# A three-stage kernel: chunk 1's router placed behind chunk 2's first product, and the loads around it reordered

## The chip, the cores and the metric

The kernel runs on one core of one Trainium2 chip. The metric is the device time of one execution in microseconds (us). The core has five engines that run side by side and wait for each other by semaphores: TensorE (matmul, "PE" in the rows), VectorE (DVE), ScalarE (ACT), GpSimd (POOL) and SyncE (SP), which here does nothing but issue DMAs. Each engine takes its instructions strictly in order, so an instruction that waits holds up all that stand behind it on its engine.

## The reference, cut to what matters

Three stages follow each other on 2304 tokens of width 512 (4 sequences of 576).

```python
# 1. attention with a window of 128 and a slope per head (8 heads of 64)
scores = q @ k.T / 8 - slope * |i - j|, masked to 0 <= i - j < 128
x = softmax(scores) @ v                      # 2304 x 512
# 2. a dense layer
h = x @ w_in                                 # 512 x 2048
y = (h * clip(h + 3, 0, 6) / 6) @ w_out      # 2048 x 512
# 3. a mixture of 8 experts, one expert per token
logits = normalise(y) @ normalise(expert_emb).T / tau
e = argmax(logits);  gate = softmax(logits)[e]
out[token] = gate * (relu(y @ w1[e]) @ w2[e])
```

Outputs are float32. The dense weights w_in and w_out come as float64, which the kernel turns into float32 itself, from their two words.

## The kernel before

The tokens are cut into nine chunks of 256 (chunk 0 to 8). For each chunk the kernel computes attention in four units (a unit is two heads of one chunk, so chunk c has units 4c to 4c+3), the first dense product in eight blocks (`gemm1`, tiles h_ps), the second product of those blocks (`gemm2`, tiles y_ps), and then the chunk's router (class `Route`). The experts come last, in the second half of the run; the change doesn't touch them.

The 16 blocks of dense weights ("pieces", 1 MB each as stored, tiles wst) are loaded and converted at the start: ScalarE and VectorE make float32 of each (`piece_clamp`, `piece_words`), and split it for later chunks into a rounded part (`piece_high`, ScalarE) and the rest (`piece_low`, VectorE, L355). Chunk 0 is computed with the plain weights (L702, L759), all later chunks as three passes over split operands (L715, L768).

Units 8 and on take their keys, queries and values by small DMAs: `load` issues those of k and q (L557), `load_v` those of v (L577, L579). VectorE turns the keys and the queries (`turn_k`, kT, and `turn_q`, qT), ScalarE scales qT, TensorE makes the scores (L605), VectorE and ScalarE the softmax, TensorE turns the weights (L644), GpSimd masks them (L659), TensorE multiplies by v (acc, L670).

A chunk's router for chunks 0 to 6 doesn't use TensorE for the logits. `rows` copies the two halves of y to ys and stores them, `norms` squares them on ScalarE and takes the root on GpSimd (rn). `spread` loads the normalised embeddings of four experts, repeated over all 128 partitions (en_all, 1 MB, L823), and `dots` runs one VectorE instruction for each expert and half of the tokens (L829, 16 in a chunk). There is one free buffer for en_all, so the second `spread` of a chunk waits for the first eight dots, and the first of the next chunk for the last eight. `choose` then takes the best expert, `ranks` counts tokens per expert on TensorE (two small matmuls into rk, L875 and L876), and `place` scatters the tokens' numbers into slots by two indirect DMAs of GpSimd (L891).

Two things set the order. Up to the end of chunk 1 a planner (`plan`) writes it out by hand: tasks with an engine, a cost, a rank, the tasks they need and the buffers they take; at each time it starts the ready task of the lowest rank, and the program takes that order on PE, ACT, DVE and SP. From then on a table of steps (`at(step, ...)`) gives TensorE's order, and a scheduler places the rest around it. Step 16.97 (`FIRST[0]`) is the first product of chunk 2, and each block takes 1.91 steps. `ends(c)` is the step at which chunk c's router begins; choose stands 10.9 steps behind it, ranks and place 12.28 (`DOTS`). For chunk 1 it returned `begins(1)`, which is 16.97 - 8 x 1.91 = 1.69. Chunk 0's router is in the planner up to its dots; its choose stands at step 16.97 and its ranks at 18.97.

In the planner, the loads of units 8 to 13 are tasks ("qk", n) with all 16 issues of a unit's keys and queries in one, and ("v", n) with its 6 or 8 issues. Those of unit 8 may begin behind the issue of piece 12 or 13, and their ranks (60 to 65) stand among those of the last pieces. `issue spread` for chunk 0 has rank 0.

Of the kernel before, what the change touches and what calls it, by code (L numbers as in the profile page):

```python
# [9 lines left out]
F32 = mybir.dt.float32  # L10
# [6 lines left out]
SP = mybir.EngineType.SP  # L17
# [35 lines left out]
UNIT_8 = (95.0, 150.0, 96.0)  # L53
EMBED = (96.0, 97.0)
SOFT_1, DOTS_0 = 250.0, 2000.0
UNIT_LOADS = ((60.0, 60.1), (61.0, 61.1), (62.0, 62.1), (63.0, 63.1), (64.0, 64.1), (65.0, 65.1))
FIRST = (16.97, 1.91, 3.35)


# [38 lines left out]
def tile_kernel(  # L98
# [13 lines left out]
    nc = tc.nc  # L112
# [27 lines left out]
    raw = right.enter_context(tc.tile_pool(name="raw", bufs=2, side="right"))  # L140
# [34 lines left out]
    for p in range(NP):  # L175
# [369 lines left out]
    class Unit:  # L545
        def __init__(self, n):
            self.c, self.p = divmod(n, NP)
            self.h0 = 2 * self.p
            self.pt, self.pp, self.nm = {}, {}, {}

        def load(self):
            def get(src, g, n, nm):
                t = raw.tile([128, n // 32, 32], F32, tag=nm, name=nm)
                for b, s, o, m in pieces_of(g, n):
                    for h in range(2):
                        for f in range(2):
                            nc.sync.dma_start(  # L557
                                out=t[64 * h + 32 * f:64 * h + 32 * f + 32, o // 32:(o + m) // 32, :],
                                in_=src[b, self.h0 + h, s:s + m, 32 * f:32 * f + 32].rearrange("(t j) i -> j t i", j=32),
                            )  # L560
                return t

            g = self.c * CH
            self.kr = get(k, g - 128, CH + 128, "kr")
            self.qr = get(q, g, CH, "qr")

        def load_v(self):
            self.vr = t = raw.tile([128, 3, 128], F32, tag="vr", bufs=V_BUFS, name="vr")
# [579 lines left out]
    n_early = EARLY_CHUNKS * NP  # L1148
# [7 lines left out]
    def begins(c, i=0):  # L1156
        return FIRST[0] + FIRST[1] * (8 * (c - 2) + i)
# [3 lines left out]
        return GROUPS[0] + GROUPS[1] * n if n < 5 else GROUPS[2] + 2 * FIRST[1] * (n - 5)  # L1161

    def ends(c, i=NF2 - 1):
        return 0.0 if c == 0 else begins(c) if c == 1 else begins(c, i) + FIRST[2]

    for c in range(2, NCH):
        for i in range(NF2):
# [6 lines left out]

    def plan():
        tasks, free = {}, {"bank": 8, "w": 17, "st": 3, "f": 5, "nm": 2, "sm": 2, "rs": 2, "ph0": 2, "ph1": 2, "g": 2,
                           "gl": 2, "u": 1, "raw": 2, "vr": 2, "kT": 1, "qT": 1, "p": 2, "part": 1, "both": 1}

        def task(name, engine, cost, rank, needs=(), takes=(), gives=(), fn=None, args=(), lag=0.12):
            assert name not in tasks, name  # L1180
# [57 lines left out]
        task(("constants",), "SP", 1.6, CONST_RANK[0], [("issue", "st", 8)], ["w"], ["w"], constants)  # L1238
        for n in range(n_early, AHEAD_UNITS):
            u = units[n]  # L1240
            for x, y in enumerate(("qk", "v") if n <= last_unit else ("qk",)):
                load((y, n), (0.6, 0.3)[x], UNIT_LOADS[n - n_early][x], ["raw" if x == 0 else "vr"], (u.load, u.load_v)[x], needs=[("issue", "st", 12 + x)] + ([("issue", y, n - 1)] if n > n_early else []), issues=(16, 6)[x])

        def step(name, engine, cost, rank, needs, takes, gives, fn, *args, lag=0.12):
            task(name, engine, cost, rank, needs, takes, gives, fn, args, lag)
# [4 lines left out]
        for n in range(n_early, last_unit + 2):  # L1250
            u, key = units[n], ("unit", n)
            first = n == n_early
            r = UNIT_8[0] if first else SOFT_1 + n
            step(key + ("kT",), "DVE", 0.5, r, [("qk", n)], ["kT"], [], u.turn_k)
            step(key + ("qT",), "DVE", 0.4, r, [key + ("kT",)], ["qT"], ["raw"], u.turn_q)
            step(key + ("scale",), "ACT", 0.45, r, [key + ("qT",)], [], [], u.scale_q)
            if n > last_unit:
                continue
            r = UNIT_8[2] if first else SOFT_1 - 10
            for h in range(2):  # L1260
                step(key + ("soften", h), "DVE", 0.85, r + 0.1 * h, [key + ("scores",)], ["p", "nm"], ["bank"], u.soften, h)
                step(key + ("expo", h), "ACT", 0.95, r + 0.2 + 0.1 * h, [key + ("soften", h)], [], ["nm"], u.expo, h)
                step(key + ("norm", h), "DVE", 0.75, r - 1, [key + ("expo", h)], ["rs"], ["rs"], u.normalise, h)
                step(key + ("unload", h), "ACT", 0.34, r - 2, [key + ("flip",)], ["ph%d" % h], ["bank"] * h, u.unload_p, h)
                step(key + ("select", h), "POOL", 1.75, r, [key + ("unload", h)], [], [], None)
            if n < last_unit:
                step(key + ("part",), "ACT", 0.36, r - 3, [key + ("values",)], ["part"], ["bank"], u.part)
                step(key + ("both",), "DVE", 0.38, r - 3, [key + ("part",)], ["both"], ["bank", "part"], u.both)
                step(key + ("keep",), "ACT", 0.36, r - 4, [key + ("both",)], [], ["both"], u.keep, lag=0.6)
                step(key + ("kept",), "DVE", 0.38, r - 4, [key + ("keep",)], [], [], None)  # L1270
# [15 lines left out]
        for x in ORDER_1:  # L1286
            before = line[-1:]
            if x == "u":
                i, at_up = at_up, at_up + 1
                name = ("up 1", i)  # L1290
                step(name, "PE", 2.88, 1000, before + [("low", ip["i", i])] + [("unit", kk, "keep") for kk in range(n_early)], ["bank"], [], gemm1, 1, i, lag=0.0)
                r = SOFT_1 - 20 + i
                step(("done 1", i), "X", 0.0, 0, [name], [], [], None, lag=0.2)
                step(("relu 1", i), "ACT", 0.62, r, [("done 1", i)], ["u"], [], relu, 1, i)
                step(("gate 1", i), "DVE", 0.62, r, [("relu 1", i)], [], ["bank"], gate, 1, i)
                step(("gh 1", i), "ACT", 0.56, r, [("gate 1", i)], ["g"], [], split_hi, 1, i)
                step(("gl 1", i), "DVE", 0.64, r, [("gh 1", i)], ["gl"], ["u"], split_lo, 1, i)
            elif x == "d":
                i, at_down = at_down, at_down + 1
                name = ("down 1", i)  # L1300
                step(name, "PE", 2.76, 1000, before + [("low", ip["o", i]), ("gl 1", i)], [] if i else ["bank", "bank"], ["g", "gl"], gemm2, 1, i, lag=0.0)
            else:
                k = int(x)
                n = n_early + k
                name = ("group flips", k)
                needs = before + both_of(("unit", n - 1, "norm")) + ([("en", "scale")] if k == 1 else [])
                step(name, "PE", 0.53 + 0.4 * (k == 1), 1000, needs, ["bank"] * (2 if k == 1 else 1), ["p", "p"] + ["f"] * (k == 1), flips_of, k, lag=0.0)
                step(("unit", n - 1, "flip"), "X", 0.0, 0, [name], [], [], None, lag=0.2)
                if k == 1:
                    step(("en", "keep"), "DVE", 0.17, SOFT_1, [name], [], ["bank"], keep_embed)  # L1310
                needs = [name, ("unit", n, "scale")] + ([("unit", n - 2, "kept")[:2] + ("select", h) for h in range(2)] + [("v", n - 2)] if k > 1 else [])
                name = ("group", k)
                step(name, "PE", 0.8 if k == 1 else 1.47, 1000, needs, ["bank"] * (2 if k == 1 else 4), ["kT", "qT"] + ["ph0", "ph1", "vr"] * (k > 1), group_of, k, lag=0.0)
                step(("unit", n, "scores"), "X", 0.0, 0, [name], [], [], None, lag=0.2)
                if k > 1:
                    step(("unit", n - 2, "values"), "X", 0.0, 0, [name], [], [], None, lag=0.1)
            line.append(name)
# [8 lines left out]
            step(("row store", t), "SP", 0.55, 0.0, [("row", t)], [], [], route_0.store, t)  # L1326
        step(("norms",), "ACT", 1.5, 1900.0, [("row", 1)], ["f"], [], route_0.norms)
        for x in range(2):
            step(("issue spread", x), "SP", 0.55, 0.0, [("en", "store")] + ([("dots", NE // 2 - 1)] if x else []), ["w"], [], route_0.spread, x)
            step(("spread", x), "DMA", 4.8, 0.0, [("issue spread", x)], [], [], None, lag=1.0)  # L1330
        for e in range(NE):
            x, y = divmod(e, NE // 2)
# [338 lines left out]
```

## Time and profile before

| what | value |
|---|---|
| time, median of 3 runs | 801.19 us (801.0 to 805.07) |
| time of the profiled execution | 807.43 us |
| its span, first to last instruction | 805.7 us |
| PE busy | 752.0 us, 93% of the span |
| DVE busy | 525.1 us, 65% |
| ACT busy | 384.1 us, 48% |
| mean granted TensorE clock | 0.976 |

The profile comes from one execution, so what it shows is measured against 807.43 us and not against the median. TensorE is busy almost throughout; the page's 40 slices show it at 7 to 9 tenths in the first fifth, then one slice at 0 and two at 8, and 9 in all but the last of the rest. Read such a profile from TensorE's gaps: a gap on the engine that is busy 93% of the time is time lost, and the view of waits says which gaps are long and what ended them. The timelines of the other engines then show why that came late.

### The profile page before, as it was taken

What the parts mean: (1) busy time and instruction counts of PE and PEld (TensorE: products, weight loads), DVE (VectorE), ACT (ScalarE), POOL (GpSimd) and SP (SyncE); (2) the same over time, 40 slices, a digit from 0 to 9 for tenths busy, and PEclk for the clock granted to TensorE, in tenths of its full rate; (3) what the DMA queues carried; (4) which work ended last, traced back from release to release, by engine and by line L of the source; (5) the groups of instructions that cost most, each with busy time, mean ns of one, the idle gap of its engine ahead of it and who ended that gap; (6) DMA issues with size and microseconds to landing.
All of it is one profiled execution on the core that took longest, in us unless ns stands there. A gap on an engine that the chain in (4) does not pass through costs nothing.

```text
span 805.7 us, 16007 instructions
## 1 busy us (share of the span) xinstructions
PE 752.0 (93%) x5740; PEld 661.9 (82%) x5740; DVE 525.1 (65%) x1528; ACT 384.1 (48%) x896; POOL 191.1 (24%) x349
## 2 busy tenths in 40 slices
PE   7999889908899999999999999999989999999995
PEld 5666568807788888888888888987979999999994
DVE  4999789866347866958777677247727537536621
ACT  6858566423345454454554544326625525535510
POOL 3010022312223224233242332113124132132200
PEclk9999989967999999999999999999999999999998
DMA  9976422262423435244334340029358565455300
GB/s 229 337 272 189 94 51 45 68 173 46 112 35 102 123 69 149 49 110 128 97 86 125 83 136 4 28 31 324 119 159 274 181 216 190 145 201 187 107 26 27
DMA packets 159110, 103.20 MB, mean 128 GB/s; under 512 B 119419, under 2 KB 135931, under 8 KB 157232
## 3 DMA queue, kind: packets, MB, share of 16 engines
q1 hardware_dynamic: 155280, 92.53, 40.2%
q0 software_dynamic: 3744, 9.58, 3.4%
q8 instruction: 47, 0.77, 0.4%
q14 instruction: 39, 0.32, 0.2%
HBM read 87.71 MB, written 14.47 MB: 127 GB/s over the span
## 4 chain that ended last, share of the span: by engine, by line
PE 61%; DMA 15%; issue 11%; DVE 4%; SPq 4%; POOL 3%; ACT 1%; POOLq 0%; DVEq 0%; ACTq 0%
PE h_ps L715 20%; PE y_ps L768 19%; PE ps_u L1038 6%; PE ps_o L1062 4%; DMA out_dram<-ob,ids 3%; DMA kr<-in_k_dram 3%; DMA wst<-in_moe_w_in_dram 3%; PE ps_z L1120 3%; PE acc L670 3%; PE sc_ps L605 2%; DMA ids<-slots 2%; DMA slots<-pays,dest 2%; DMA xg<-ybuf,ids 2%; PE ps_pt L644 1%; SPq L557 1%
## 5 line engine op out<-in xcount | busy, mean ns | idle before, releaser
L715 PEld LDWEIGHTS h_ps<-xs,w_i 128*128 128x128 f32 x1536 | 194.4, 193 | 5.8 <-issue 0.8
L715 PE MATMUL h_ps<-xs,w_i 128*128 128x256 f32 x1536 | 197.2, 285 | 0.0
L768 PE MATMUL y_ps<-w_o,gh 128*128 128x512 f32 x512 | 162.9, 399 | 0.5 <-ACT gh L739 0.5
L659 POOL TENSOR_SCALAR_AFFINE_SELECT ph<-ph 64x128 f32<-64x128 f32 x224 | 90.5, 404 | 194.5 <-ACT ph L651 153.2
L768 PEld LDWEIGHTS y_ps<-w_o,gh 128*128 128x128 f32 x512 | 91.6, 188 | 24.5 <-issue 6.3
L1038 PE MATMUL ps_u<-x,w_e 128*128 128x280 f32 (+5 forms) x768 | 105.4, 294 | 0.0
L162 DVE TENSOR_TENSOR w_e<-st,w_e 128x1024 fp32r<-128x1024 f32 x64 | 76.5, 1217 | 38.4 <-ACT w_e L161 38.4
L1038 PEld LDWEIGHTS ps_u<-x,w_e 128*128 128x128 f32 x768 | 100.5, 189 | 0.2
L768 PE MATMUL y_ps<-w_o,gl 128*128 128x512 f32 x256 | 100.1, 391 | 0.4 <-DVE gl L745 0.4
L829 DVE CUSTOM_DVE_ANT_0 junk<-ys,en_all 128x512 f32<-128x512 f32 x112 | 77.3, 690 | 30.4 <-DMA en_all<-en_rows 18.7
L725 ACT ACTIVATE u<-h_ps,three 128x512 f32<-128x512 f32 x72 | 49.1, 682 | 75.4 <-PE h_ps L715 54.2
L1062 PE MATMUL ps_o<-hs,w_e 128*128 128x280 f32 (+4 forms) x576 | 78.5, 295 | 0.0
L735 DVE SCALAR_TENSOR_TENSOR u<-u,h_ps 128x512 f32<-128x512 f32 x72 | 49.3, 684 | 43.8 <-ACT u L725 42.9
L1062 PEld LDWEIGHTS ps_o<-hs,w_e 128*128 128x128 f32 x576 | 76.6, 188 | 0.0
L161 ACT CAST w_e<-st 128x1024 fp32r<-128x1024 f32 x64 | 65.5, 1048 | 17.1 <-DMA st<-in_moe_w_dram 6.3
L739 ACT CAST gh<-u 128x512 fp32r<-128x512 f32 x64 | 39.7, 620 | 59.4 <-DVE u L735 58.8
L745 DVE TENSOR_TENSOR gl<-u,gh 128x512 fp32r<-128x512 f32 x64 | 45.7, 714 | 27.7 <-ACT gh L739 27.0
L628 ACT ACTIVATE pt<-pt,nm 128x128 f32<-128x128 f32 x112 | 44.1, 395 | 31.4 <-DVE pt L621 31.3
L768 PEld LDWEIGHTS y_ps<-w_o,gl 128*128 128x128 f32 x256 | 48.1, 188 | 11.9 <-DVE gl L745 1.2
L1137 POOL DMA_INDIRECT out_dram<-ob,ids x23 | 30.3, 1315 | 111.8 <-DVE ob L1136 100.3
L1046 ACT ACTIVATE hs<-ps_u 128x280 fp32r<-128x280 f32 (+5 forms) x64 | 25.6, 403 | 45.4 <-PE ps_u L1038 44.8
L891 POOL DMA_INDIRECT slots<-pays,dest x18 | 19.8, 1098 | 95.8 <-DVE u L735 36.4
(185 smaller groups left out, 1007.9 us busy)
## 6 DMA issues: line engine op xcount, KB each, us to landing
st<-in_moe_w_dram SPq DMA_DIRECT2D x32, 512.0 KB
st<-in_moe_w_dram SPq DMA_DIRECT2D x16, 1024.0 KB
en_all<-en_rows SPq DMA_DIRECT2D x14, 1024.0 KB
wst<-in_moe_w_in_dram SPq DMA_DIRECT2D x8, 1024.0 KB
wst<-in_moe_w_out_dram SPq DMA_DIRECT2D x8, 1024.0 KB
ybuf<-ys SPq DMA_DIRECT2D x18, 256.0 KB
out_dram<-empty SPq DMA_DIRECT2D x18, 256.0 KB
kr<-in_k_dram SPq DMA_DIRECT2D x48, 48.0 KB
```

Of the source, the lines that this page charges most:

```text
L161: nc.scalar.copy(hi, src)
L162: eng.tensor_tensor(out=lo, in0=src, in1=words(hi), op=ALU.subtract)
L628: nc.scalar.activation(out=x, in_=x, func=AF.Exp, scale=-1.0, bias=nm[:, j:j + 1], accum_out=sums[h][:, j:j + 1])
L659: nc.gpsimd.affine_select(out=out, in_=x, compare_op=ALU.is_gt if out is prev else ALU.is_ge, fill=0.0, base=0, pattern=[[0, 2], [-1 if ou ...
L715: nc.tensor.matmul(hp[:, f, :], lhsT=w[:, a, kk, f * 128:(f + 1) * 128], rhs=xs[:, b, kk, :], start=(n == 0), stop=(n == 3 * KD - 1),)
L725: nc.scalar.activation(out=u, in_=hp, func=AF.Relu, bias=three, scale=1.0)
L735: V.scalar_tensor_tensor(out=u, in0=u, scalar=6.0, in1=h_t[c, i], op0=ALU.min, op1=ALU.mult)
L745: V.tensor_tensor(out=gl, in0=g, in1=words(gh), op=ALU.subtract)
L768: nc.tensor.matmul(y_t[c][t], lhsT=g[a][:, f, t * 128:(t + 1) * 128], rhs=w[:, b, f, :], start=(i == 0 and f == 0 and n == 0), stop=(i == ...
L829: V.tensor_tensor_reduce(out=self.junk, in0=self.ys[t], in1=self.en[:, e % (NE // 2), :], scale=1.0, scalar=0.0, op0=ALU.mult, op1=ALU.add ...
L1038: nc.tensor.matmul(ps, lhsT=w[:, a, kk, (f % 2) * 128:(f % 2) * 128 + 128], rhs=x[:, b, kk, c0:c1], start=(n == 0), stop=(n == 3 * KD - 1),)
L1062: nc.tensor.matmul(ps, lhsT=ws_t[j, 4 + f // 2][:, a, f % 2, d * 128:(d + 1) * 128], rhs=hs[:, b, f, 0:width(j)], start=(n == 0), stop=(n ...
```

## The change

There are three edits. First, `ends(1)` returns `begins(2)`, 16.97, in the place of `begins(1)`, 1.69: chunk 1's rows, norms, spreads, dots, choose, ranks and place stand 15.28 steps later in the table. Second, `Unit.load` is cut into `load_k` and `load_q`, and the planner has three tasks for each unit (keys, queries, values), with costs of their own and buffers kr and qr counted apart; unit 8's may begin behind the issue of pieces 12 and 13 as before, those of all later units behind piece 15, the last. Third, the spreads of chunk 0 have rank 90 in the place of 0 and also need piece 15 to be issued.

```diff
-UNIT_LOADS = ((60.0, 60.1), (61.0, 61.1), (62.0, 62.1), (63.0, 63.1), (64.0, 64.1), (65.0, 65.1))
+UNIT_LOADS = (80.0, 81.0, 82.0, 83.0, 84.0, 85.0)
...
+        def load_k(self):
+            self.kr = self.get(k, self.c * CH - 128, CH + 128, "kr")
+
+        def load_q(self):
+            self.qr = self.get(q, self.c * CH, CH, "qr")
...
     def ends(c, i=NF2 - 1):
-        return 0.0 if c == 0 else begins(c) if c == 1 else begins(c, i) + FIRST[2]
+        return 0.0 if c == 0 else begins(2) if c == 1 else begins(c, i) + FIRST[2]
...
-            for x, y in enumerate(("qk", "v") if n <= last_unit else ("qk",)):
-                load((y, n), (0.6, 0.3)[x], UNIT_LOADS[n - n_early][x], ["raw" if x == 0 else "vr"], (u.load, u.load_v)[x], needs=[("issue", "st", 12 + x)] + ([("issue", y, n - 1)] if n > n_early else []), issues=(16, 6)[x])
+            for x, y in enumerate(("rk", "rq", "rv") if n <= last_unit else ("rk", "rq")):
+                late = ("issue", "st", 12 + x if n == n_early else 15)
+                load((y, n), (0.43, 0.29, 0.15)[x], UNIT_LOADS[n - n_early] + 0.1 * x, [("kr", "qr", "vr")[x]], (u.load_k, u.load_q, u.load_v)[x], needs=[late] + ([("issue", y, n - 1)] if n > n_early else []), issues=(8, 8, 6)[x])
...
-            step(("issue spread", x), "SP", 0.55, 0.0, [("en", "store")] + ([("dots", NE // 2 - 1)] if x else []), ["w"], [], route_0.spread, x)
+            step(("issue spread", x), "SP", 0.55, 90.0, [("en", "store"), ("issue", "st", 15)] + ([("dots", NE // 2 - 1)] if x else []), ["w"], [], route_0.spread, x)
```

What this moves shows in the order of the instructions. TensorE behind chunk 1's last product (the first two rows are its last matmuls; rk is a router, ps_pt, acc and sc_ps are one group of attention), before:

```order
L768 MATMUL y_ps<-w_o,gh 128x512 x2
L768 MATMUL y_ps<-w_o,gl 128x512
L875 LDWEIGHTS earlier
L875 MATMUL rk<-oh,earlier 128x16
L876 LDWEIGHTS ones
L876 MATMUL rk<-seen,ones 128x16
L715 MATMUL h_ps<-xs,w_i 128x256 x48
...
L644 MATMUL ps_pt<-ident,pt 128x2x64 x4
```

and in the change:

```order
L773 MATMUL y_ps<-w_o,gh 128x512 x2
L773 MATMUL y_ps<-w_o,gl 128x512
L720 MATMUL h_ps<-xs,w_i 128x256 x48
L880 LDWEIGHTS earlier
L880 MATMUL rk<-oh,earlier 128x16
L881 LDWEIGHTS ones
L881 MATMUL rk<-seen,ones 128x16
L649 MATMUL ps_pt<-ident,pt 128x2x64 x4
L675 MATMUL acc<-ph,vr 64x192 x4
L675 MATMUL acc<-ph,vr 64x128 x4
L675 MATMUL acc<-ph,vr 64x64 x4
L610 MATMUL sc_ps<-kT,qT 64x192 x8
```

Before, the first rk is chunk 1's; the second, chunk 0's, follows the 48 matmuls of chunk 2's first two blocks. In the change only one router stands here, chunk 0's, behind the 48 matmuls, and chunk 1's follows some 60 rows later, behind five more blocks of h_ps, five of y_ps and three groups of attention. The sc_ps of this group are unit 14's.

SyncE from the store of the normalised embeddings to the last piece, before:

```order
L285 DMA en_rows<-en 8x512
L823 DMA en_all<-en_rows 128x2048
L315 DMA wst<-in_moe_w_out_dram 128x2x1024
L315 DMA wst<-in_moe_w_in_dram 128x4x512
L315 DMA wst<-in_moe_w_out_dram 128x2x1024
L557 DMA kr<-in_k_dram 32x6x32 x8
...
L315 DMA wst<-in_moe_w_in_dram 128x4x512
...
L315 DMA wst<-in_moe_w_out_dram 128x2x1024
...
L579 DMA vr<-in_v_dram 128x64 x2
L315 DMA wst<-in_moe_w_out_dram 128x2x1024
```

and in the change:

```order
L285 DMA en_rows<-en 8x512
L315 DMA wst<-in_moe_w_out_dram 128x2x1024
L315 DMA wst<-in_moe_w_in_dram 128x4x512
L315 DMA wst<-in_moe_w_out_dram 128x2x1024
L562 DMA kr<-in_k_dram 32x6x32 x8
L315 DMA wst<-in_moe_w_in_dram 128x4x512
...
L315 DMA wst<-in_moe_w_out_dram 128x2x1024
...
L584 DMA vr<-in_v_dram 128x64 x2
L315 DMA wst<-in_moe_w_out_dram 128x2x1024
```

Before, the spread of 1 MB stood ahead of the last six pieces, and unit 8's 16 key and query loads, its eight value loads and all 24 loads of unit 9 ahead of the last of them. In the change the spread stands 13 rows behind the last piece, behind the loads of units 9, 10 and 11, and only unit 8's loads are left ahead of it, cut in three between the last pieces.

VectorE around the gate u of chunk 0's last block and chunk 1's first gl (w_i and w_o are the low parts of split pieces, L333 to L339 the conversion of the last piece), before:

```order
L333 TENSOR_SCALAR w_909<-w_909 128x1024
L589 STREAM_TRANSPOSE qT<-qr 128x256
L335 SCALAR_TENSOR_TENSOR w_909<-wst,w_909 128x1024
L355 TENSOR_TENSOR w_i<-w_364,w_i 128x1024
L339 SCALAR_TENSOR_TENSOR w_909<-wst,w_909 128x1024
L735 SCALAR_TENSOR_TENSOR u<-u,h_ps 128x512
L355 TENSOR_TENSOR w_i<-w_505,w_i 128x1024
L355 TENSOR_TENSOR w_o<-w_724,w_o 128x1024
L735 SCALAR_TENSOR_TENSOR u<-u,h_ps 128x512
L355 TENSOR_TENSOR w_o<-w_550,w_o 128x1024
L745 TENSOR_TENSOR gl<-u,gh 128x512
```

and in the change:

```order
L740 SCALAR_TENSOR_TENSOR u_994<-u_994,h_ps_875 128x512
L355 TENSOR_TENSOR w_i_923<-w32_424,w_i_923 128x1024
L355 TENSOR_TENSOR w_i_1013<-w32_364,w_i_1013 128x1024
L355 TENSOR_TENSOR w_i_1016<-w32_505,w_i_1016 128x1024
L355 TENSOR_TENSOR w_o_1019<-w32_664,w_o_1019 128x1024
L355 TENSOR_TENSOR w_o_1050<-w32_550,w_o_1050 128x1024
L355 TENSOR_TENSOR w_i_1061<-w32_550,w_i_1061 128x1024
L740 SCALAR_TENSOR_TENSOR u_1068<-u_1068,h_ps_1021 128x512
L355 TENSOR_TENSOR w_i_1071<-w32_664,w_i_1071 128x1024
L355 TENSOR_TENSOR w_o_1074<-w32_747,w_o_1074 128x1024
L750 TENSOR_TENSOR gl_1112<-u_1068,gh_1077 128x512
```

Before, the last piece's conversion stood directly ahead of the last gate, five low parts stood somewhere ahead of it and three between it and gl. In the change the conversion is some 20 rows further ahead, three low parts stand ahead of the gate and eight between it and gl.

VectorE ahead of unit 14's queries, in the change (junk is a dot of chunk 1, lg its sum, u and gl are chunk 2's second block, both, xs unit 12's):

```order
L740 SCALAR_TENSOR_TENSOR u<-u,h_ps 128x512
L834 ISA junk,lg<-ys,en_all 128x512
L834 ISA lg 128x1
...
L689 TENSOR_TENSOR both<-acc,part 128x256
L750 TENSOR_TENSOR gl<-u,gh 128x512
L590 STREAM_TRANSPOSE kT<-kr 128x384
L893 CAST dest<-den 128x2
L162 TENSOR_TENSOR xs<-both,xs 128x256
L834 ISA junk,lg<-ys,en_all 128x512
...
L594 STREAM_TRANSPOSE qT<-qr 128x256
```

Four dots of chunk 1 stand ahead of unit 14's keys and four more between its keys and its queries. Before, its keys stood behind eight dots and its queries behind eleven, and TensorE had not begun chunk 2 by then.

## Rows read from the trace of the kernel before

**Rows 1.** windows view: stretch, length, then PE PEld DVE ACT POOL busy, clock, DMA share, GB/s
```profile
103.00:162.00 59.00, 58.54 (x472) 48.05 (x472) 52.35 (x151) 34.05 (x85) 16.90 (x41) 0.95 0.24 56
162.00:215.00 53.00, 26.74 (x215) 23.68 (x216) 29.19 (x123) 13.95 (x41) 10.99 (x32) 0.74 0.41 98
```

**Rows 2.** the waits view, TensorE, first 260 us: total, times, longest
```profile
PE rk L875 <- DVE oh L866: 23.6, 1, 23.6
PE y_ps L759 <- DVE u L735: 4.7, 1, 4.7
PE acc L670 <- POOL ph L659: 3.1, 2, 1.8
```

**Rows 3.** timeline of TensorE, 160 to 216 us: start, us, what, wait before
```profile
161.16 0.39 PE L768 MATMUL y_ps<-w_o,gl 128*128 128x512 f32 x1
...
185.43 8.12 PE L715 MATMUL h_ps<-xs,w_i 128*128 128x256 f32 x48
...
193.46 0.64 PE L644 MATMUL ps_pt<-ident,pt 128*128 128x128 f32 x4
...
195.49 0.73 PE L768 MATMUL y_ps<-w_o,gh 128*128 128x512 f32 x2
...
203.99 3.03 PE L715 MATMUL h_ps<-xs,w_i 128*128 128x256 f32 x24
206.86 0.60 PE L644 MATMUL ps_pt<-ident,pt 128*128 128x128 f32 x4
...
214.22 0.73 PE L768 MATMUL y_ps<-w_o,gh 128*128 128x512 f32 x2
```

**Rows 4.** timeline of VectorE, 160 to 184 us
```profile
160.42 0.42 DVE L684 TENSOR_TENSOR both<-acc,part 128x256 f32<-128x256 f32 x1
...
164.73 0.17 DVE L868 TENSOR_SCALAR rn<-rn 128x2 f32<-128x2 f32 x1 [1.27 <-POOL rn L818]
...
177.82 0.69 DVE L829 CUSTOM_DVE_ANT_0 junk<-ys,en_all 128x512 f32<-128x512 f32 x1 [4.92 <-DMA en_all<-en_rows]
...
178.56 0.69 DVE L829 CUSTOM_DVE_ANT_0 junk<-ys,en_all 128x512 f32<-128x512 f32 x1
```

**Rows 5.** timeline of SyncE's DMA issues, 51 to 173 us
```profile
51.40 0.32 SPq L823 DMA_DIRECT2D en_all<-en_rows  x1
...
53.59 11.11 SPq L557 DMA_DIRECT2D kr<-in_k_dram  x8
...
70.05 0.39 SPq L315 DMA_DIRECT2D wst<-in_moe_w_in_dram  x1
...
76.23 0.38 SPq L315 DMA_DIRECT2D wst<-in_moe_w_out_dram  x1
...
90.79 0.38 SPq L315 DMA_DIRECT2D wst<-in_moe_w_out_dram  x1
...
172.44 0.34 SPq L823 DMA_DIRECT2D en_all<-en_rows  x1
```

**Rows 6.** timeline of TensorE, 90 to 112 us
```profile
90.68 3.60 PE L759 MATMUL y_ps<-w,u 128*128 128x512 f32 x8
...
94.78 3.22 PE L715 MATMUL h_ps<-xs,w_i 128*128 128x256 f32 x24
102.74 6.47 PE L759 MATMUL y_ps<-w,u 128*128 128x512 f32 x8 [4.74 <-DVE u L735]
...
111.92 0.63 PE L768 MATMUL y_ps<-w_o,gh 128*128 128x512 f32 x2
```

**Rows 7.** timeline of VectorE, 97 to 104 us
```profile
97.66 0.69 DVE L333 TENSOR_SCALAR w<-w 128x1024 int32<-128x1024 int32 x1 [4.96 <-ACT w L323]
...
102.00 0.68 DVE L735 SCALAR_TENSOR_TENSOR u<-u,h_ps 128x512 f32<-128x512 f32 x1
102.60 1.22 DVE L355 TENSOR_TENSOR w_i<-w,w_i 128x1024 fp32r<-128x1024 f32 x1
103.73 1.22 DVE L355 TENSOR_TENSOR w_o<-w,w_o 128x1024 fp32r<-128x1024 f32 x1
```

More of the change, by code (lines that the diff above doesn't have):

```diff
@@ L549, in __init__, with get @@
             self.pt, self.pp, self.nm = {}, {}, {}
-        def load(self):
[L552 to L565, printed above, removed]
+        def load_k(self):
+            self.kr = self.get(k, self.c * CH - 128, CH + 128, "kr")
+        def load_q(self):
+            self.qr = self.get(q, self.c * CH, CH, "qr")
+        def get(self, src, g, n, nm):
+            t = raw.tile([128, n // 32, 32], F32, tag=nm, name=nm)
+            for b, s, o, m in pieces_of(g, n):
+                for h in range(2):
+                    for f in range(2):
+                        nc.sync.dma_start(
+                            out=t[64 * h + 32 * f:64 * h + 32 * f + 32, o // 32:(o + m) // 32, :],
+                            in_=src[b, self.h0 + h, s:s + m, 32 * f:32 * f + 32].rearrange("(t j) i -> j t i", j=32),
+                        )
+            return t
+        def load(self):
+            self.load_k()
+            self.load_q()
         def load_v(self):
@@ L1176, in plan @@
         tasks, free = {}, {"bank": 8, "w": 17, "st": 3, "f": 5, "nm": 2, "sm": 2, "rs": 2, "ph0": 2, "ph1": 2, "g": 2,
-                           "gl": 2, "u": 1, "raw": 2, "vr": 2, "kT": 1, "qT": 1, "p": 2, "part": 1, "both": 1}
+                           "gl": 2, "u": 1, "kr": 2, "qr": 2, "vr": 2, "kT": 1, "qT": 1, "p": 2, "part": 1, "both": 1}
         def task(name, engine, cost, rank, needs=(), takes=(), gives=(), fn=None, args=(), lag=0.12):
@@ L1253, in plan @@
             r = UNIT_8[0] if first else SOFT_1 + n
-            step(key + ("kT",), "DVE", 0.5, r, [("qk", n)], ["kT"], [], u.turn_k)
-            step(key + ("qT",), "DVE", 0.4, r, [key + ("kT",)], ["qT"], ["raw"], u.turn_q)
+            step(key + ("kT",), "DVE", 0.5, r, [("rk", n)], ["kT"], ["kr"], u.turn_k)
+            step(key + ("qT",), "DVE", 0.4, r, [key + ("kT",), ("rq", n)], ["qT"], ["qr"], u.turn_q)
             step(key + ("scale",), "ACT", 0.45, r, [key + ("qT",)], [], [], u.scale_q)
@@ L1310, in plan @@
                     step(("en", "keep"), "DVE", 0.17, SOFT_1, [name], [], ["bank"], keep_embed)
-                needs = [name, ("unit", n, "scale")] + ([("unit", n - 2, "kept")[:2] + ("select", h) for h in range(2)] + [("v", n - 2)] if k > 1 else [])
+                needs = [name, ("unit", n, "scale")] + ([("unit", n - 2, "kept")[:2] + ("select", h) for h in range(2)] + [("rv", n - 2)] if k > 1 else [])
                 name = ("group", k)
```

## The prediction

> **What bounds the kernel now.** I read the page first: TensorE is busy 93% of the span, so time is lost where it is not. The windows view then cuts the run into stretches [rows 1]. From 103 to 162 us, chunk 1's products, TensorE is busy 58.54 of 59 us; from 162 to 215, the start of chunk 2, 26.74 of 53, at a granted clock of 0.74. The view of waits names the gaps [rows 2]: 23.6 us for the router's rk, once, 4.7 us for a gate (u) of chunk 0's last block, 3.1 us for masked weights (ph). The reader is to see that three waits hold nearly all that can be won here.
>
> The large one, on the timeline: chunk 1's last product ends at 161.16 + 0.39 = 161.55, and the next 48 matmuls start at 185.43, behind the router [rows 3]. VectorE shows what the router waits for [rows 4, 5]: chunk 0's last dot ends at 160.42; only then can chunk 1's first spread go. Its dots need the second spread too, issued at 172.44; the first dot behind it begins at 177.82, 5.4 us later, and dots follow each other by 0.74. So chunk 1's chain of two spreads and 16 dots is bare, while TensorE has chunk 2's first blocks ready behind it.
>
> The loss is larger than the wait. From 161.55 to the third y_ps block of chunk 2 at 214.22 are 52.7 us [rows 3]. The work in it, at the full-speed steps of the same rows: the 48 matmuls 2 x 2.87 (203.99 to 206.86) = 5.7; a group of attention 193.46 to 195.49 = 2.0, twice; two blocks of each product, 195.49 to 206.86 = 11.4; two routers 0.4. That is 21.5, so 31.2 are lost: 23.6 waiting; 2.2 because the 48 matmuls take 8.0 (185.43 to 193.46) in place of 5.7 and 0.1 of router; and 5.3 in the second group, 7.4 (206.86 to 214.22) in place of 2.0, of which 3.1 are the wait for ph [rows 2] and the rest a slow restart.
>
> The early gap: TensorE ends chunk 1's first block at about 94.78 + 2.87 = 97.7 and stands until 102.74 [rows 6]. It waits for the gate at 102.00, which VectorE reaches late because it stood still for 4.96 us until 97.66, for the conversion of the last piece [rows 7]. That piece was issued at 90.79, 14.6 us behind the one before it, with unit 9's loads between [rows 5].
>
> **The change part by part.** *Chunk 1's router.* It moves behind five more blocks of each product and three groups. Chunk 0's is now first, behind the 48 matmuls; its dots are done 1.1 us before chunk 1 ends [rows 3, 4], so it waits for nothing. Chunk 1's rk now stands 5.7 + 10 x 2.8 + 3 x 2.0 = 40 us of TensorE's work behind chunk 1, against a chain of 24; I cost it at nothing. All 31.2 of the stretch can go: the wait, the restart and also the 5.3, since two routers' scatters no longer stand together ahead of a group's masks on GpSimd, and the masks for this group now come first there.
>
> *What is late next.* The first group behind the 48 matmuls makes unit 14's scores. Before, unit 14's loads, turns and scaling lay under the long wait. Now VectorE has four of chunk 1's dots ahead of unit 14's kT and four between kT and qT. From the end of chunk 1 (0): the first spread is issued at -1.1 and lands 5.4 later by the second one's row, at +4.3 [rows 4, 5]. Ahead of the dots also stands rn, which came at 164.73 = +3.2; it now waits for a square placed behind the clip of chunk 2's first block (product 2.9, clip, square, root at about 0.7 to 0.8 each by instructions of that size), some +5.6. From there eight dots 5.9, a gate 0.6, two gl 1.3, kT, qT, both and xs 1.7, small ones 0.3: +15.4; scaling 0.5: +15.9. TensorE is through at 5.7 + 0.2 + 1.3 = +7.2 or so (the group's turn and values are 1.3 of its 2.0): a new wait of 8.6. Bounds: 7.4 if rn costs nothing and the landing decides; 15 if the spread lands as late as the eight key loads took to issue behind other large loads, 11.1 [rows 5], in place of 5.4, plus a little for the queue. I take 8.6, since both spreads have the same size and neighbours.
>
> *The restart.* Behind 23.6 us of waiting the restart cost 2.2; behind 4.7 us, the eight y_ps take 6.47 in place of 3.60, or 2.9 [rows 3, 6]. 8.6 lies between; I take 2.5. A price in proportion to the wait would be 8.6/23.6 x 2.2 = 0.8. The Trainium skill (TensorE: Matmul & The Clock Gate, Why this matters for your kernels) says that an idle gap between bursts puts the array back to half rate, a price for each gap and not for its length. The trace agrees: 2.9 behind the shorter wait, 2.2 behind the longer. By the skill the stage gives 31.2 - 8.6 - 2.5 = 20.1, by proportion 21.8; I keep 20.1, which the rows give alone.
>
> *Pieces ahead of loads.* Without unit 9's loads ahead, the last piece goes at about 76 at the latest, in place of 90.79; without the spread's 1 MB (issued at 51.40) and its wait earlier still. VectorE then loses its idle 4.96. It also has three low parts of split pieces ahead of the last gate, five before: 2 x 1.13 less [rows 7]. The gate falls to 102.0 - 5.0 - 2.3 = 94.7. But now six low parts stand between it and the next gate, and two more ahead of gl: 0.6 + 8 x 1.13 + 0.6 = 10.2, so gl stands at 104.9, and chunk 1's first y_ps, whose third matmul needs it, starts at 104.5 in place of 111.92 [rows 6]: 7.4 won. TensorE alone would allow 97.7 + 3.4 + 2.9 = 104.0, 7.9. Lower bound: -2, if the loads that stayed ahead (unit 8's) hold the pieces as before and the eight low parts come on top. I take 7.4, as VectorE's own instructions set it and no transfer I can see comes later. From there chunk 1 runs on a full TensorE [rows 1], so the gain is carried.
>
> *The later loads and spread.* Units 9 to 11 load in some 31 us behind the last piece, by about 105, and the spread follows; chunk 0's dots were not begun before 111, and its router isn't due before 162. Nothing. The issues are the same in number; they only change places. Behind chunk 2's start all engines have the same order within a chunk, so the rest moves as a whole.
>
> *Sum.* 20.1 + 7.4 = 27.5. The profiled execution takes 807.43, the median is 801.19, 6.2 less; 801.2 - 27.5 = 773.7.
>
> **The rivals.** *The pieces come no earlier, or VectorE pays for its low parts elsewhere* (0.14): only 20.1 is won, 781. For it: the key loads took 11.1 us to issue while large transfers were under way [rows 5], and they still stand ahead of three pieces. Against: that queue is shorter by the spread, and unit 9 is out.
>
> *Unit 14 is later than I say* (0.14): landing at the far bound, a wait of 15 and perhaps a second restart: 774 + 9 = 783. For it: its 8 loads stand right behind the 1 MB spread on the one queue. Against: kT stands behind four dots anyway, so keys have until +11.
>
> *No wait at unit 14* (0.04): dots begun early, 8.6 + 2.5 won more, 763. Against it: the dots need the spread, and it can't go before chunk 0's last dot.
>
> *The router still stops TensorE* (0.02): chunk 0's rk waits as chunk 1's did, if its second spread slips by 20 us behind the loads now ahead of it; some 794, and within 0.5% only if the early gain fails too.
>
> *Slower* (0.04): chunk 1's dots stand among chunk 2's gates on VectorE, and an instruction that waits for a spread holds up the gates behind it. If both halves are bare there, TensorE pays two landings of 5.4, 16 dots of 0.74 and three restarts of 2.5: 30; with unit 14's 11.1 and the 5.3 of masks behind scatters 46 against 38.6 taken away (31.2 and 7.4): 809. It decides once the second spread lands after the gate of chunk 2's fifth block. Against: the second spread is due about +20, its dots stand behind two more groups.
>
> **How the numbers follow.** Likeliest, 0.62: 774, on its own 769 to 780. The range is 764 to 787: it takes in the far bounds of the early term (781) and of unit 14 (783), with a few us on top where both fall together, and leaves out most of the case without a wait, the slower one and the one where the router still stops TensorE. A measurement of this kernel can tell about 0.5%, 4 us, from no change. Faster by that: 0.94 (the first four cases but for a few tails); within: 0.02; slower: 0.04.
>
> **What would show it.** Right: the profile after has no wait of TensorE for rk above 1 us; chunk 1 ends near 154; the one large wait is sc_ps of unit 14 on qT, 7 to 10 us, with a slow y_ps behind it; no wait of 4 us for a gate near 100. Wrong: a wait for rk at chunk 0's router, a wait of ScalarE for the last piece as long as before, or TensorE waiting for gates of chunk 2 behind a dot that waits for en_all.

## The result, and the profile after

The changed kernel takes 778.44 us (median of 4 runs, 776.51 to 778.85), beside 801.38 us of the kernel before on the same chip (801.0 to 805.07): a ratio of 0.970, 95% interval 0.967 to 0.973. The forecast was 774, within 764 to 787. The profiled execution takes 778.85, its span is 777.1 us, its mean granted clock 0.989. Lines of the code are five further down than before.

The windows view, two stretches as long as those of [rows 1] (length, PE PEld DVE ACT POOL busy, clock, DMA share, GB/s):

```profile
95.00:154.00 59.00, 58.25 (x493) 49.42 (x492) 54.16 (x151) 34.32 (x85) 18.95 (x40) 1.00 0.31 75
154.00:207.00 53.00, 45.09 (x375) 39.68 (x374) 40.34 (x167) 23.17 (x70) 15.02 (x40) 0.90 0.43 109
```

The second stretch had 26.74 us of TensorE's work at a clock of 0.74 and now has 45.09 at 0.90. The view of waits of TensorE in the first 260 us (us in total, times, longest), the rows that answer [rows 2]:

```profile
PE sc_ps L610 <- ACT qT L601: 7.9, 1, 7.9
...
PE y_ps L773 <- DVE gl L750: 0.8, 1, 0.8
```

The waits for rk, for the gate of chunk 0's last block and for ph are gone; one large wait is left, that of unit 14's scores. TensorE's timeline from the end of chunk 1 to the end of chunk 2's third y_ps block (start, us, what, wait before), beside [rows 3]:

```profile
153.46 0.39 PE L773 MATMUL y_ps<-w_o,gl 128*128 128x512 f32 x1
153.68 5.91 PE L720 MATMUL h_ps<-xs,w_i 128*128 128x256 f32 x48
159.44 0.18 PE L880 MATMUL rk<-oh,earlier 128*128 128x16 bf16 x1
...
160.07 0.89 PE L675 MATMUL acc<-ph,vr 64*64 64x192 f32 x24
168.86 1.56 PE L610 MATMUL sc_ps<-kT,qT 64*64 64x192 f32 x16 [7.91 <-ACT qT L601]
170.35 1.22 PE L773 MATMUL y_ps<-w_o,gh 128*128 128x512 f32 x2
...
174.60 3.04 PE L720 MATMUL h_ps<-xs,w_i 128*128 128x256 f32 x24
...
183.09 0.60 PE L649 MATMUL ps_pt<-ident,pt 128*128 128x128 f32 x4
...
184.33 0.83 PE L610 MATMUL sc_ps<-kT,qT 64*64 64x192 f32 x16
185.09 0.74 PE L773 MATMUL y_ps<-w_o,gh 128*128 128x512 f32 x2
...
187.99 3.04 PE L720 MATMUL h_ps<-xs,w_i 128*128 128x256 f32 x24
```

Chunk 1 ends at 153.46 + 0.39 = 153.85, before at 161.55. From there to the start of the third y_ps block (185.09) are 31.24 us, before 52.67. Chunk 0's router (rk, 159.44) waits for nothing. VectorE in the same stretch, beside [rows 4]:

```profile
158.87 0.17 DVE L873 TENSOR_SCALAR rn<-rn 128x2 f32<-128x2 f32 x1 [0.16 <-POOL rn L823]
...
159.19 0.69 DVE L834 CUSTOM_DVE_ANT_0 junk<-ys,en_all 128x512 f32<-128x512 f32 x1
...
163.13 0.41 DVE L689 TENSOR_TENSOR both<-acc,part 128x256 f32<-128x256 f32 x1
...
164.06 0.56 DVE L590 STREAM_TRANSPOSE kT<-kr 128x384 f32<-128x384 f32 x1
...
164.93 0.77 DVE L834 CUSTOM_DVE_ANT_0 junk<-ys,en_all 128x512 f32<-128x512 f32 x1
...
167.83 0.44 DVE L594 STREAM_TRANSPOSE qT<-qr 128x256 f32<-128x256 f32 x1
```

ScalarE then scales the queries, and unit 14's scores follow:

```profile
168.30 0.51 ACT L601 ACTIVATE qT<-qT,units_of 128x256 f32<-128x256 f32 x1 [4.32 <-DVE lg L834]
```

The first dot stands behind rn, four dots are through before unit 14's keys are turned (164.06), four more before its queries (167.83). Neither turn has a wait in front of it (there is no bracket in its row), so VectorE came to them late and didn't wait there for unit 14's loads. The early part, TensorE beside [rows 6]:

```profile
96.89 3.60 PE L764 MATMUL y_ps<-w,u 128*128 128x512 f32 x8
...
103.19 0.63 PE L773 MATMUL y_ps<-w_o,gh 128*128 128x512 f32 x2
104.58 0.50 PE L773 MATMUL y_ps<-w_o,gl 128*128 128x512 f32 x1 [0.75 <-DVE gl L750]
```

Chunk 1's first y_ps starts at 103.19 (111.92 before) with a wait of 0.75 inside, since the last piece is issued at 73.16 and not at 90.79 [rows 5].

### The profile page after: what moved, and what is told of

It is laid out like the page before. It is cut to its first block, busy times and chain, and to the rows that moved or that the text cites. A ratio compares the mean times of both kernels' runs of the same rounds, so it can differ in the third digit from the quotient of the medians.

```text
span 777.1 us, 15993 instructions
## 1 busy us (share of the span) xinstructions
PE 748.5 (96%) x5740; PEld 659.8 (85%) x5740; DVE 522.6 (67%) x1528; ACT 383.8 (49%) x896; POOL 195.7 (25%) x349
## 4 chain that ended last, share of the span: by engine, by line
PE 67%; DMA 11%; DVE 8%; issue 7%; SPq 3%; ACT 2%; POOL 1%; POOLq 0%; DVEq 0%; ACTq 0%
PE y_ps L773 21%; PE h_ps L720 21%; PE ps_u L1043 7%; PE ps_o L1067 4%; PE ps_z L1125 3%; PE acc L675 3%; DMA out_dram<-ob,ids 2%; PE sc_ps L610 2%; DMA ids<-slots 2%; DMA xg<-ybuf,ids 2%; DMA wst<-in_moe_w_out_dram 2%; DMA slots<-pays,dest 2%; PE ps_pt L649 1%; SPq L562 1%; DVE w L335 1%
## 5 line engine op out<-in xcount | busy, mean ns | idle before, releaser
L720 PEld LDWEIGHTS h_ps<-xs,w_i 128*128 128x128 f32 x1536 | 192.4, 191 | 6.1 <-issue 1.2
L720 PE MATMUL h_ps<-xs,w_i 128*128 128x256 f32 x1536 | 195.2, 283 | 0.0
L664 POOL TENSOR_SCALAR_AFFINE_SELECT ph<-ph 64x128 f32<-64x128 f32 x224 | 95.5, 426 | 193.9 <-ACT ph L656 156.6
L1052 DVE SCALAR_TENSOR_TENSOR hs<-ps_u,hs 128x280 fp32r<-128x280 f32 (+5 forms) x64 | 27.8, 443 | 20.6 <-ACT hs L1051 20.2
```

The costliest lines, as they stand in the source:

```text
L664: nc.gpsimd.affine_select(out=out, in_=x, compare_op=ALU.is_gt if out is prev else ALU.is_ge, fill=0.0, base=0, pattern=[[0, 2], [-1 if ou ...
L720: nc.tensor.matmul(hp[:, f, :], lhsT=w[:, a, kk, f * 128:(f + 1) * 128], rhs=xs[:, b, kk, :], start=(n == 0), stop=(n == 3 * KD - 1),)
```

## The experiments

Each is timed against the kernel before on the same chip; intervals are 95%. The kernel before had a median of 800.17 us beside the first four runs, 798.65 beside the next four, 797.57 beside the three after these and 797.54 beside the last.

**One edit alone.** The first edit:

```diff
-        return 0.0 if c == 0 else begins(c) if c == 1 else
+        return 0.0 if c == 0 else begins(2) if c == 1 else
```

> The kernel before with the first edit alone (chunk 1's router 15.28 steps later). Theory A, the prediction's: the two gains are separate, and this one takes the stage at chunk 2's start alone: the wait for rk (23.6 us) goes, a wait of 7 to 9 us of unit 14's scores and its slow restart (2 to 3) come, chunk 1 still ends near 161.5: 20 to 21 us faster, 780 to 781. Theory B: the profiled execution of the kernel before, 6.2 us over the median, had its surplus in this stage, so less is won against the median: 786. Theory C: moving the router back pays only because unit 14's keys come early enough by the other edits; here the wait for unit 14 is 15 us or more: 788.

Measured 781.76, ratio 0.978 (0.973 to 0.982): 18.4 us, by the interval 14 to 21. The wait for rk is gone and unit 14's is 7.9 us, so the new wait doesn't come from the moved loads; theory C is out. A and B both lie in the interval. The second and third edit alone (the diff of the change without that line):

> The second and third edits alone (loads in three tasks, spread behind the last piece); chunk 1's router stays where it was before. Theory A: chunk 1 ends near 154 and carries the chain of its router along, since that chain starts at chunk 0's last dot, which VectorE reaches in its order: the wait for rk stays at 22 to 25 us, 7.4 us faster, 794. Theory B: chunk 0's dots hang on the spread, which now goes last, so the chain does not move with chunk 1 and the wait for rk grows by what chunk 1 wins, to about 31 us: 801.

Measured 790.88, ratio 0.990 (0.987 to 0.993): 9.3 us, by the interval 5 to 11. The wait for rk is 23.6 again: the chain moved along with chunk 1. Theory A.

**Which of the two early edits.** The third undone, then the second:

```diff
-0.55, 90.0, [("en", "store"), ("issue", "st", 15)] + ([("dots"
+0.55, 0.0, [("en", "store")] + ([("dots"
```

> The changed kernel with its third edit undone: chunk 0's first spread (1 MB) goes ahead of the last pieces again. Theory A: what held the last piece was unit 9's loads, which stay out of the way; the spread costs the pieces its own transfer, about 3.6 us at 279 GB/s, so the early gain of 7.7 falls to about 4 and the time is 782. Theory B: the spread does not matter: 778. Theory C: the early gain needs both edits: chunk 1 ends near 161 and the time is 786.

```diff
-            for x, y in enumerate(("rk", "rq", "rv") if n <= last_unit else ("rk", "rq")):
+            for x, y in enumerate(("qk", "v") if n <= last_unit else ("qk",)):
```

> The changed kernel with its second edit undone: unit loads are two tasks with the old ranks, so unit 9's 22 issues stand ahead of the last piece again, while the spread stands behind it. Theory A: the last piece goes at 88 to 91 instead of 73, VectorE and ScalarE wait for it, and the gate near 100 is late again: chunk 1 ends near 161, 785 to 786. Theory B: the spread was what held the pieces: chunk 1 ends near 155, 779.

Measured 777.94 (0.973, 0.968 to 0.978) and 777.13 (0.972, 0.968 to 0.977): neither loses anything. In time it is theory B both times. The last product of chunk 1 in the two profiled executions:

```profile
153.91 0.39 PE L773 MATMUL y_ps<-w_o,gl 128*128 128x512 f32 x1
153.57 0.39 PE L768 MATMUL y_ps<-w_o,gl 128*128 128x512 f32 x1
```

Chunk 1 ends at 154.30 and 153.96, with all three edits at 153.85. In the second of the two unit 9's loads do stand ahead of the last piece, which is issued at 85.56; ScalarE's row of its conversion (the wait for it in brackets; in the kernel before 5.94 us until 96.48):

```profile
90.63 1.16 ACT L323 ACTIVATE w<-wst 128x1024 f32<-128x1024 f32 x1 [0.45 <-DMA wst<-in_moe_w_out_dram]
```

Without the spread ahead the piece goes 5.2 us earlier than at 90.79, and no more was needed. The other way, with the spread ahead and unit 9 behind, it goes at 76.69. Either edit alone gives the early gain; the two are not added.

**The kernel before once more.** No edit.

> The kernel before once more, for a second profiled execution. Theory A: the first profiled execution of the kernel before stood 6.2 us over the median because its early gap was longer than usual (4.7 us of wait for the gate and 2.9 of slow restart); here, in an execution near the median of 800 to 801, that wait is 0 to 3 us, chunk 1's first y_ps starts 3 to 5 us earlier than 111.92, while the wait for rk stays at 23 to 24. Theory B: the early gap is the same in every execution and the surplus sits at chunk 2's start: chunk 1's first y_ps starts near 111.9, and the wait for rk is 19 to 21 us.

Measured 798.52, ratio 1.001 (0.999 to 1.003); the profiled execution's span is 797.1 us, 8.6 less than the first one's. TensorE's timeline, beside [rows 3, 6]:

```profile
101.47 5.40 PE L759 MATMUL y_ps<-w,u 128*128 128x512 f32 x8 [3.33 <-DVE u L735]
...
109.58 0.63 PE L768 MATMUL y_ps<-w_o,gh 128*128 128x512 f32 x2
...
158.81 0.39 PE L768 MATMUL y_ps<-w_o,gl 128*128 128x512 f32 x1
182.96 0.19 PE L875 MATMUL rk<-oh,earlier 128*128 128x16 bf16 x1 [23.76 <-DVE oh L866]
...
204.67 0.60 PE L644 MATMUL ps_pt<-ident,pt 128*128 128x128 f32 x4
...
205.91 1.00 PE L670 MATMUL acc<-ph,vr 64*64 64x192 f32 x19 [0.18 <-POOL ph L659]
...
207.72 0.73 PE L768 MATMUL y_ps<-w_o,gh 128*128 128x512 f32 x2
```

Neither theory as it stands. The early gap is shorter, as A says, but by less: the gate's wait is 3.33 in place of 4.74, chunk 1's first y_ps 2.3 us earlier, its end at 159.20 in place of 161.55. The wait for rk is the same, 23.8. The stage differs too, as B says, though not in that wait: 207.72 - 159.20 = 48.52 in place of 52.67, and the 4.15 us lie in the second group, 3.05 us here (204.67 to 207.72) and 7.36 in [rows 3], where it waited 3.1 us for masks. In this execution that wait is 0.18. GpSimd's row of the masks, in the first execution and here:

```profile
208.60 5.68 POOL L659 TENSOR_SCALAR_AFFINE_SELECT ph<-ph 64x128 f32<-64x128 f32 x15 [7.59 <-DMA slots<-pays,dest]
203.78 5.27 POOL L659 TENSOR_SCALAR_AFFINE_SELECT ph<-ph 64x128 f32<-64x128 f32 x13 [6.99 <-issue]
```

Both times the scatters of the two routers stand ahead of the masks on GpSimd, as the prediction has it. In the first execution chunk 0's scatter began 9.55 us behind the end of chunk 1's, and GpSimd stood another 7.59 us between that scatter with a first mask and the other masks; here it is 7.38 and 6.99. Why the scatters took longer there stays open. (The last 2.1 of the 8.6 us lie in the second half of the run, where gathered rows were waited for 4.1 us in the first execution and 1.4 here.)

**What makes the wait of unit 14.** One number moves chunk 1's first spread behind unit 14's loads, and by that its turns ahead of all dots:

```diff
-                    at(g + loads[x], r.spread, x)
+                    at(g + loads[x] + 0.1 * (c == 1), r.spread, x)
```

> The changed kernel, with chunk 1's first spread a tenth of a step later, which puts unit 14's loads ahead of it on SyncE and kT and qT of unit 14 ahead of all dots on VectorE. Theory A (VectorE's order makes the wait of 7.9 us): the scaled qT comes some 4.4 us earlier, at about 164.4 instead of 168.8, the wait of unit 14's scores falls to 3 to 4 us, the restart still costs about 2; 774. Theory B (the transfers of unit 14 make it): the wait stays at 7 to 8 and the time at 778. If the price of a restart goes with the length of the wait, it falls to about 1 us and the time is 773.

TensorE's waits, and its timeline behind unit 12's values and at chunk 1's router:

```profile
PE sc_ps L610 <- ACT qT L601: 3.4, 2, 3.2
...
PE rk L880 <- DVE oh L871: 2.2, 1, 2.2
```

```profile
164.27 0.88 PE L610 MATMUL sc_ps<-kT,qT 64*64 64x192 f32 x16 [3.22 <-ACT qT L601]
165.08 0.73 PE L773 MATMUL y_ps<-w_o,gh 128*128 128x512 f32 x2
...
167.93 3.04 PE L720 MATMUL h_ps<-xs,w_i 128*128 128x256 f32 x24
...
200.33 0.17 PE L880 MATMUL rk<-oh,earlier 128*128 128x16 bf16 x1 [2.22 <-DVE oh L871]
...
200.63 1.20 PE L773 MATMUL y_ps<-w_o,gh 128*128 128x512 f32 x2
```

The scores start at 164.27, the wait falls to 3.2: theory A for the cause, VectorE's order. The run puts the loads ahead as well as the turns, so by itself it couldn't tell the two apart; the changed kernel's rows of VectorE above, with no wait at either turn, do. Two things were not expected. Behind these 3.2 us nothing is slow (scores 0.81, y_ps block 2.85). This execution, of 774.32 us, is the fastest of the five and its mean granted clock is 0.994; the others took 776.34 to 777.43 at 0.990 or 0.991, so a restart may well have been paid there, though not shown. And the dots that went behind unit 14 now come late for chunk 1's own router: rk waits 2.2 us at 200.33, and the block behind it, which ends at 204.89, takes 4.26 in place of 2.85. The time is 777.11 (774.32 to 777.43; ratio 0.973, 0.971 to 0.975), not the 774 forecast.

**The price of the restart.**

```diff
+            if n == AHEAD_UNITS:
+                at(t0, warm, 30)
             at(t0, u.scores)
```

> The changed kernel with 30 matmuls of 128x128 whose result nobody uses, put between unit 12's values and unit 14's scores on TensorE, where it waits 7.9 us; at the 0.22 to 0.23 us of one at full clock they take 6.6 to 6.9 us. Theory A (the slow scores and slow first y_ps behind the wait are a price of TensorE having stood still): the granted clock stays at 1.0, sc_ps takes 0.8 instead of 1.5, the y_ps block 2.75 instead of 4.25, 2.2 us faster, 776. Theory B (they are slow because of what else runs then, such as loads and dots): no change, 778.

```profile
160.03 6.97 PE L411 MATMUL warm<-ident 128*128 128x128 f32 x60
168.02 0.88 PE L610 MATMUL sc_ps<-kT,qT 64*64 64x192 f32 x16 [1.02 <-issue]
...
171.69 3.04 PE L720 MATMUL h_ps<-xs,w_i 128*128 128x256 f32 x24
```

The windows view of the changed kernel's wait and of the scores and y_ps block behind it, and of this kernel's:

```profile
161.00:168.90 7.90, 0.04 (x4) 0.04 (x4) 7.17 (x24) 2.62 (x7) 6.12 (x10) 0.64 0.63 143
168.90:174.60 5.70, 5.70 (x28) 4.18 (x29) 3.63 (x19) 1.65 (x8) 0.00 (x0) 0.61 0.18 26
```

```profile
160.00:167.00 7.00, 7.00 (x68) 6.78 (x60) 6.90 (x24) 2.27 (x6) 5.17 (x10) 1.00 0.67 159
168.00:172.00 4.00, 3.98 (x31) 3.19 (x32) 2.59 (x15) 1.65 (x8) 0.00 (x0) 1.00 0.21 34
```

Theory A: with idle work in the gap the granted clock stays at 1.00 (2.4 GHz), and scores and block (168.02 to 171.69) take 3.67 us instead of 5.74, 2.1 less. Measured 775.42 (775.3 to 778.97), ratio 0.972 (0.970 to 0.975): by the time alone it can't be told from the changed kernel, by the rows it can.

**A better order.** Besides the line of the spread, unit 14's loads earlier and its group one block later:

```diff
-            at(t0 - early, u.load)
+            at(t0 - early - 1.5 * (n == AHEAD_UNITS), u.load)
...
-... else GROUPS[2] + 2 * FIRST[1] * (n - 5)
+... else GROUPS[2] + 2 * FIRST[1] * (n - 5) + 1.35 * (n == 6)
```

> The changed kernel, with unit 14's loads 1.5 steps earlier and chunk 1's spread a tenth later (unit 14's kT and qT ahead of all dots), and the group of unit 14's scores 1.35 steps later, behind one more y_ps block and one more h_ps block of chunk 2. Theory A: TensorE has work until about 167 us when the scores come, qT is scaled by then, no wait over 1.5 us is left at chunk 2's start except for the first gate (about 1); with the restart 8 to 9 us are won: 769 to 770, faster than both kernels. Theory B: chunk 1's dots come so late that the second spread and chunk 1's router stop TensorE later, at rk, or the group's values hold up a later one: 775 or more.

```profile
PE ps_pt L649 <- DVE pt L643: 4.2, 2, 3.1
...
PE rk L880 <- DVE oh L871: 1.6, 1, 1.6
```

Measured 774.08 (773.13 to 776.95), ratio 0.971 (0.968 to 0.973). Unit 14's wait is gone, but the dots now stand among unit 14's softmax, and TensorE waits 4.2 us for its weights (ps_pt) and 1.6 for rk. The time lies between the two theories; for most of what was hoped for, B holds. The same kernel and the changed one side by side, and a version with chunk 1's dots and router later:

```diff
-                    at(g + halves[x][0] + halves[x][1] * y, r.dots, e)
+                    at(g + halves[x][0] + halves[x][1] * y + 2.2 * (c == 1 and x == 0), r.dots, e)
...
-            at(g + d2 * (c > 0), r.choose)
+            at(g + d2 * (c > 0) + 2.0 * (c == 1), r.choose)
```

(ranks and place 2.0 later as well.)

> The changed kernel once more, beside the next two, and for a second profiled execution. Theory A: what moved between executions of the kernel before (the early gap, the second group's masks) is gone in the changed kernel, so its times lie within 3 us, 776 to 779, and the wait of unit 14's scores is 7.9 us again. Theory B: the changed kernel moves as much as the kernel before (8 us between the lowest and the highest).

> The version with unit 14 ahead of the dots and its group one block later, again, to be timed beside the changed kernel. Theory A: what it wins at unit 14 (7.9 us of wait and 2.2 of restart) less what it loses later (4.2, 1.3 and 1.6) is 3 us: 774 to 775 against 777 to 778. Theory B: no difference.

> The version with unit 14 ahead of the dots and its group one block later, and besides it chunk 1's first eight dots 2.2 steps later and its choose, ranks and place 2 steps later. Theory A: the wait of 4.2 us for unit 14's weights (its softmax stood between eight dots on VectorE), the slow group behind it (1.3) and the wait of 1.6 for rk all go: 5 to 7 us less than that version, 767 to 769. Theory B: the dots only move on to the next unit's softmax and TensorE waits there: 772 to 775.

The changed kernel: 777.04 (775.33 to 778.57), ratio 0.974 (0.972 to 0.976), its wait 7.9 again; theory A, it moves by 3 us. The version of before: 775.49 (774.51 to 776.55), ratio 0.973 (0.971 to 0.975): 1.6 us better, and the intervals overlap. The last one tells nothing of the time: only four of its first eight dots stand ahead of the second spread, so the other four read the other half of the embeddings, the logits of two experts are others, and some 1265 of its 2088 us are a later part of the program that doesn't appear in the other profiles. With the second spread and its dots moved along:

```diff
+                    at(g + loads[x] + (0.1, 2.2)[x] * (c == 1), r.spread, x)
+                    at(g + halves[x][0] + halves[x][1] * y + (2.2, 1.6)[x] * (c == 1), r.dots, e)
```

> As e11_router_later, but with the second spread and its dots moved along (by 2.2 and 1.6 steps), so that every dot reads its own half of the embeddings; in e11_router_later two dots of the first half stood behind the second spread and read the wrong ones. Theory A: the wait for unit 14's weights falls from 4.2 to 1 or 2 us (six dots among its softmax in place of eight, and four of them behind it), the wait for rk goes: 768 to 771, faster than all versions so far. Theory B: the dots only move on and TensorE waits for the next unit's weights or for chunk 2's gates: 773 to 776.

```profile
PE ps_pt L649 <- DVE pt L643: 1.4, 2, 1.0
PE sc_ps L610 <- ACT qT L601: 1.1, 1, 1.1
```

Measured 770.5 (769.9 to 771.93), ratio 0.967 (0.964 to 0.970). The waits of 4.2 and 1.6 became 1.4, rk isn't waited for, and 1.1 us for the next unit's scores came in. No run of it is as slow as the fastest of the changed kernel (775.33), which was timed on another chip. By the ratios, each taken on one chip, its interval lies below that of the changed kernel's second timing (0.972 to 0.976) and overlaps that of the first (0.967 to 0.973). So it very likely beats the changed kernel too: theory A.

## Why the prediction was right, and where its size was off

*The wait for rk.* Right: it goes, and chunk 1's router, at 204.25, waits for nothing. "I cost it at nothing" holds, but with little to spare: where the dots moved behind unit 14, rk waited 2.2 and 1.6 us.

*The new wait.* Right in place, cause and size: 7.91 against 8.6. The first dot begins 5.3 us behind chunk 1's end (forecast 5.6, and rn is what it waits for), qT is scaled at +15.0 (forecast +15.9). That VectorE's order makes it is shown by the turns, which wait for nothing, and by turning the order round.

*The restart.* 2.1 against 2.5: the scores take 1.49 instead of 0.76, the y_ps block 4.25 instead of 2.90 (184.33 to 187.99). That it is the price of standing still was shown by the filler. The Trainium skill (TensorE: Matmul & The Clock Gate, Why this matters for your kernels) was quoted for a price of each gap; its row speaks only of gaps above a certain length. The 3.2 us without any price contradict the quotation, and the gaps of 2.2 and 2.6 us with one, shown below, contradict the row. So 2.5 was near the size for this gap, not a rule.

*The stage.* 52.67 - 31.24 = 21.4 against 20.1, in the executions compared. As forecast, the masks of the first group come ahead of the scatters on GpSimd now (at 161.61 and 166.16).

*The early gain.* 161.55 - 153.85 = 7.7 against 7.4, gl is through at 103.84 + 0.68 = 104.52 against 104.9. The reason holds (with unit 9's loads out and the spread still ahead the piece goes at 76.69, forecast about 76), but it is not the only way: without the spread's 1 MB ahead, the piece comes early enough with unit 9's loads in place.

*The sum.* Here the forecast is off: 22.9 us were measured, 27.5 forecast. The step that failed is "The profiled execution takes 807.43, the median is 801.19, 6.2 less; 801.2 - 27.5". It takes a gain worked out in one execution from the time of others. Within that execution the terms hold: 21.4 + 7.7 = 29.1, and the profiled times differ by 807.43 - 778.85 = 28.6. But in it chunk 1 ended 2.35 us later than in the second execution of the same kernel and the stage was 4.15 longer: 6.5 us, about its surplus of 6.2, and both lay in waits that the change removes. The other runs agree that it was the unusual one. With the loads alone, where rk is still waited for, the stage takes 48.2 us; with the router alone, where the early part is the old one, chunk 1 ends at 158.15. Against the second execution the terms are 159.20 - 153.85 = 5.35 and 48.52 - 31.24 = 17.3, together 22.6. That this meets the 22.9 so closely is in part luck. The profiled times of these two executions differ by only 798.93 - 778.85 = 20.1, because behind the stage the changed kernel's took 2.6 us longer: it waited 4.7 us for gathered rows, the other 1.4, and this wait lies anywhere between 1.4 and 4.7 in the kept executions, whatever the edit. The changed kernel's second timing gives 797.57 - 777.04 = 20.5. The forecast would have been 807.43 - 27.5 = 779.9 had the sum been taken from the profiled time itself. The term most over-sized for a usual execution is "the 5.3": with masks that came in time the second group loses 3.05 - 2.0 = 1.05.

## What to carry to other kernels

Before a wait is booked as a gain, ask whether it is there in every execution: a profiled execution that is 6 us over the median has its 6 us somewhere, and if that is in the waits to be removed, the sum belongs to the profiled time. When a long chain is moved behind other work, it brings its instructions along on each engine: look for the first thing that now stands behind them (here two turns behind eight dots), and put it ahead. When a transfer comes late, take away from ahead of it only as much as it is late; here 5.2 us were enough, and the 17.6 of the whole change (73.16 against 90.79) won no more.

## What the runs showed of the hardware

A gap of TensorE does not have one price. Behind the 7.9 us of unit 14's wait, scores and y_ps block took 5.74 us in the changed kernel, 5.11 in its second execution and 6.17 to 6.54 in the kernels with one edit undone or done alone, in place of 3.66 at full clock: 1.4 to 2.9 us for the same gap. Behind 3.2 us nothing was lost in the execution that was profiled (granted clock 1.00). Yet later in that same execution, behind 2.2 us, a y_ps block took 4.26 us in place of 2.85, and behind 2.6 us, in the kernel with the first edit alone, 4.83 in place of 3.03. Its timeline and its windows:

```profile
100.42 5.40 PE L759 MATMUL y_ps<-w,u 128*128 128x512 f32 x8 [2.57 <-DVE u L735]
105.25 3.44 PE L715 MATMUL h_ps<-xs,w_i 128*128 128x256 f32 x24
```

```profile
100.40:105.30 4.90, 4.88 (x9) 2.08 (x9) 4.90 (x6) 3.27 (x5) 0.00 (x0) 0.65 0.29 46
105.30:110.00 4.70, 4.70 (x33) 4.20 (x32) 2.92 (x6) 3.53 (x7) 1.23 (x1) 1.00 0.45 135
```

Over those 4.9 us the granted clock was 0.65 on the average, part of them at the lower of its two levels (1.2 and 2.4 GHz); from 94.64 to 97.85 TensorE had worked without a gap. So neither a fixed price for each gap nor one by its length fits. What decided between the 2.2 and the 3.2 us stays open.
